# Interleaving a pair's two heads by row in the transposed scores, and making their pads on GpSimd

## The chip, the cores and the metric

The kernel runs on one core of a Trainium2 chip. A core has five engines that work side by side, each with its own queue of instructions: TensorE (PE) multiplies matrices and writes its results to PSUM; VectorE (DVE), ScalarE (ACT) and GpSimd (POOL) work on tiles in SBUF, and the first two on PSUM too; SyncE (SP) issues nearly all of this kernel's DMA transfers between SBUF and HBM. They are ordered against each other by semaphores only. Before a matmul TensorE loads a weight tile of up to 128x128 (the row PEld), which overlaps with the matmul before it.

The metric is the device time of the kernel in microseconds (us); lower is better.

## The reference, cut to what matters

Two mixers over the same 2048 rows of 512 features are blended by a gate:

```python
g = sigmoid((x * gate_w).sum(-1, keepdims=True))
a = Real(DFT_seq(DFT_hid(x)))            # matmuls with four DFT matrices
b = windowed_attention(x, wqkv, wo)      # 32 heads of 16, window 256, causal
out = g * a + (1 - g) * b

# inside b, for each head:
scores = q @ k.T * 16 ** -0.5
mask = (i - j >= 0) & (i - j < 256)
p = softmax(where(mask, scores, -1e9)); o = p @ v
```

All of it is float32. The change concerns the attention alone.

## The kernel before, in words

**Heads and steps.** The 32 heads are taken as four groups `g` of four pairs `p` of two heads `h`. A step `n` is one block of 64 rows of one group: 4 x 32 = 128 steps. In a step each pair's two heads share one matmul. For this, a *pad* is made: a 128x128 weight tile per pair in which 64 columns hold head 0's data (and zeros in head 1's feature rows) and the other 64 columns hold head 1's. With the pad as weights and the whole ring of keys or queries streaming, one matmul gives the scores of both heads, head 0 in partitions 0 to 63, head 1 in 64 to 127.

**Two passes.** `s_pair(n, p)` computes scores by query: pad of q (`pads[0]`), up to 320 keys (line 356); VectorE adds the mask and takes the row's extremum (358), ScalarE the exponentials with their sum (361). Nineteen steps later (`LAG`), `t_pair(k, p)` computes the same scores transposed, by key: pad of k (`pads[1]`), up to 320 queries (439). The row extremum comes in through extra rows 96 to 99 of the ring of q (written back from DRAM), and extra rows of the pad of k hold ones for the head they belong to (`mrow`, 208). ScalarE's exponential then writes the probabilities `pt` (440). GpSimd zeroes with `affine_select` what the window excludes: the first 64 queries (445) and, for a full window, the last 64 (449). This is done after each second pair (`p` odd) for two pairs at once, separately for each head's 64 partitions.

**The product with v.** `v_load` brings four blocks of v by two DMAs, head 0 to partitions 0 to 63, head 1 to 64 to 127; `v_spread` copies each half on GpSimd into its own 16 columns of `vpad` (423), whose other columns were zeroed once (203). `pv` (466) multiplies `vpad` with `pt` for the steps finished, three to five steps after their t, four pairs in four column stripes of TensorE.

**Pads.** `make_pad(i, n)` (332 to 340) is called for pad n one step ahead. Each pad is two instructions, one for each head, multiplying by the 0/1 column `half`. VectorE makes all of them (339) but the second half of the t pads, which ScalarE makes (337). There are two buffers for each kind, so pad n overwrites the pad of step n-2.

**What sets the order.** TensorE's order is written out by hand (`manual_schedule`): in the loop over n and p, `s_pair`, a quota of matmuls of the dense stream (`fill`: projections, then the DFT over rows, `dc`, line 518), `t_pair`, and again a quota; 16 dense matmuls a step while s runs, 12 after it. After step 127 of s only t and the dense stream remain for 19 steps, and then the DFT and the output projection alone. The orders on VectorE, ScalarE, GpSimd and SP come from a planner that simulates the engines; a few instructions are tied behind others (`behind`).

Of the kernel before, what the change touches and what calls it, by code (L numbers as in the profile page):

```python
# [7 lines left out]
F32 = mybir.dt.float32  # L8
F32R = mybir.dt.float32r
AF = mybir.ActivationFunctionType  # L10
OP = mybir.AluOpType
# [3 lines left out]
P = 128  # L15
# [5 lines left out]
BQ = 64  # L21
NB = S // BQ
WIN = 320
# [9 lines left out]
def fnet_window_mix(ctx: ExitStack, tc: tile.TileContext, xT, x, wqk, wv, wr, wi, cr, ci, wo, gw, out):  # L33
    nc = tc.nc

    const = ctx.enter_context(tc.tile_pool(name="const", bufs=1))
# [11 lines left out]
    v_scr = [dram.tile([2, P, 2, NG, 64], F32, name=f"v_scr{i}") for i in range(8)]  # L48
# [6 lines left out]
    def ld(dst, src):  # L55
        mark("sp", nc.sync.dma_start(dst, src))

    def f(ap):
        return ap.bitcast(F32)
# [4 lines left out]
    def mark(e, ins):  # L64
        last[e] = ins.ins

    @contextmanager
    def behind(*engines):
        with ExitStack() as es:
            for e in engines:  # L70
                if e in last:
                    es.enter_context(tc.issue_after(last[e]))
            yield
# [68 lines left out]
    with tc.manual_schedule(engines={mybir.EngineType.Activation, mybir.EngineType.DVE, mybir.EngineType.SP}):  # L142
# [12 lines left out]
        for dk in range(DK):  # L155
            c = slice(dk * 256, dk * 256 + 256)
# [7 lines left out]
    ring = [const.tile([P, NP, S], F32R, name=f"ring{i}") for i in range(2)]  # L164
# [3 lines left out]
    for h in (0, 64):  # L168
        m = mask[h:h + 64, :]
        nc.gpsimd.affine_select(m, m, pattern=[[1, WIN]], compare_op=OP.is_gt, fill=BIG,  # L170
                                base=0, channel_multiplier=-1)
        nc.gpsimd.affine_select(m, m, pattern=[[-1, WIN]], compare_op=OP.is_ge, fill=BIG,
                                base=256, channel_multiplier=1)
    ident = const.tile([P, P], F32R, name="ident")
    nc.gpsimd.memset(f(ident[:]), 1.0)
    nc.gpsimd.affine_select(ident[:], f(ident[:]), pattern=[[1, P]], compare_op=OP.is_equal, fill=0.0,
                            base=0, channel_multiplier=-1)

    half = const.tile([P, 2], F32, name="half")
    mrow = const.tile([P, 2], F32, name="mrow")  # L180
    for t, edges in ((half, ((0, 16, 32, 48, 64, 80), (16, 32, 48, 64, 80, 96))), (mrow, ((96, 98), (98, 100)))):
        nc.gpsimd.memset(t, 0.0)
        for h in range(2):
            for i, e in enumerate(edges[h]):
                a = t[:, h:h + 1]
                nc.gpsimd.affine_select(a, a, pattern=[[0, 1]], compare_op=OP.is_ge, fill=1.0 - i % 2,
                                        base=e - 1, channel_multiplier=-1)

    def clear_rows(i, ss):
        with behind("pool"):  # L190
            nc.gpsimd.memset(f(ring[i][96:128, :, ss * 512:(ss + 1) * 512]), 0.0)

    first_lo = f(XT[0, 0][96:128, 1]).rearrange("r (p c) -> r p c", p=NP)
    for t in pads[0]:
        mark("pool", nc.gpsimd.affine_select(t[96:128], first_lo, pattern=[[0, NP], [0, P]], compare_op=OP.is_gt,
                                             fill=0.0, base=0, channel_multiplier=0))
    clear_rows(1, 0)
    clear_rows(0, 0)
    vpad = [const.tile([P, 4, NP, 32], F32, name=f"vpad{b}") for b in range(2)]

    def clear_pads():
        for t in vpad:
            nc.gpsimd.memset(t, 0.0)
        for t in pads[1]:
            nc.gpsimd.memset(f(t[96:128]), 1.0)
            for h in range(2):
                a = t[96:128, :, 64 * h:64 * h + 64]
                nc.vector.tensor_scalar(a, f(a), mrow[96:128, h:h + 1], None, op0=OP.mult)


# [117 lines left out]
    def make_pad(i, n):  # L328
        if not 0 <= n < NG * NB:
            return  # L330
        t = pads[i][n % NPAD]
        b = n % NB
        with behind(*(("act", "dve") if n < NPAD else ())):
            for h in range(2):
                src, dst = f(ring[i][:96, :, b * BQ:(b + 1) * BQ]), t[:96, :, 64 * h:64 * h + 64]
                if i and h:
                    nc.scalar.activation(dst, src, AF.Copy, scale=half[:96, h:h + 1])  # L337
                else:
                    nc.vector.tensor_scalar(dst, src, half[:96, h:h + 1], None, op0=OP.mult)  # L339
        PAD[i, n] = t  # L340

    ML = {}
# [63 lines left out]
    def v_load(n):  # L406
        if n >= NG * NB:
            return
        g, kb = divmod(n, NB)
        raw = at.tile([P, 4, 64], F32, name="vr", bufs=1)  # L410
        for h in range(2):
            ld(raw[64 * h:64 * h + 64].rearrange("r (c j) x -> r c j x", j=2),
               v_scr[kb // 4][:, :, h, g, :].rearrange("c (j r) x -> r c j x", r=64))
        VR[n] = raw

    def v_spread(n):
        if n >= NG * NB:
            return
        raw = VR.pop(n)
        v2 = vpad[n // 4 % 2]  # L420
        for h in range(2):
            r = slice(64 * h, 64 * h + 64)
            nc.gpsimd.tensor_copy(v2[r, :, :, 16 * h:16 * h + 16], raw[r].rearrange("r j (p d) -> r j p d", d=16))  # L423
        V2[n // 4] = v2

    def t_pair(n, p):
        q0 = n % NB * BQ
        w = min(WIN, S - q0)
        if p == 0:
            if "proj" in have:  # L430
                more.append(n)
            c = (n - more[0]) % 6 * NP * WIN if more else 3072
            if c + NP * WIN <= 3072:
                PT[n] = f(home[:, c:c + NP * WIN].rearrange("p (a b) -> p a b", a=NP))
            else:
                PT[n] = at.tile([P, NP, WIN], F32, name="pt", bufs=4)
        pt = PT[n]
        ps = ps_a.tile([P, 512], F32, name="t", tag="st")
        nc.tensor.matmul(ps[:, :w], PAD[1, n][:, p], ring[0][:, p, q0:q0 + w], start=True, stop=True)  # L439
        nc.scalar.activation(pt[:, p, :w], ps[:, :w], AF.Exp, scale=-1.0)  # L440
        if p % 2:
            ph = slice(p - 1, p + 1)
            for h in (0, 64):
                a = pt[h:h + 64, ph, 0:64]
                nc.gpsimd.affine_select(a, a, pattern=[[0, 2], [1, 64]], compare_op=OP.is_ge, fill=0.0,  # L445
                                        base=0, channel_multiplier=-1)
                if w == WIN:
                    a = pt[h:h + 64, ph, 256:320]
                    nc.gpsimd.affine_select(a, a, pattern=[[0, 2], [-1, 64]], compare_op=OP.is_gt, fill=0.0,  # L449
                                            base=0, channel_multiplier=1)  # L450

    def pv(n):
        g, kb = divmod(n, NB)
# [375 lines left out]
    def v_next(n):  # L829
        if n < N:  # L830
            for c in range(2):
                need(("v", n % NB // 2 + c))
            with behind(*(("sp",) if n < 8 else ())):
                v_load(n)

    for n in range(N + LAG + 1):
# [3 lines left out]
        if n == 7:  # L840
            clear_pads()
        k = n - LAG
        ring_ahead(n + 1)
        if k in (-1, 4):
            v_spread(0 if k < 0 else 4)
        if k in (-4, -1, 4):
            v_next({-4: 0, -1: 4, 4: 8}[k])
        if n == 0:
            make_pad(0, 0)
        for p in range(NP):  # L850
            if n < N:
                s_pair(n, p)
            fill(n)
            if 0 <= k < N:
                t_pair(k, p)
            if p == 0:
                make_pad(0, n + 1)
                if k >= -1:
                    make_pad(1, k + 1)
            fill(n)  # L860
            for at_n, at_p, do in TURN:
                u, j = divmod(n - at_n, 8)
                if p == at_p and j == 0 and 0 <= u < 16:
                    do(u)
            if p == 3 and k % 8 == 6 and 0 <= k < N:
                l_load(k // 8)
            if p == 0 and full:
                o_out()
            if p == 2 and (k - summed >= (5 if more else 3) or k == N):
                for j in range(summed, k):  # L870
                    pv(j)
                summed = k
            if p == 3 and 4 * spread - 5 < summed and 4 * spread < N and n >= fresh:
                v_spread(4 * spread)
                spread += 1
                v_next(4 * spread)
                fresh = n + 2
# [49 lines left out]
```

## Time and profile before

| | |
|---|---|
| time, median of 3 runs | 855.69 us (852.19 to 856.47) |
| profiled execution, first to last instruction (span) | 854.1 us; the page gives no other time of it |
| busy: TensorE, VectorE, ScalarE, GpSimd | 844.2, 618.1, 592.0, 372.6 us |
| granted TensorE clock | 1.000 |
| t matmuls run | from 100.9 to 763.5 us |
| DMA | 161.04 MB, mean 189 GB/s |

A row of the profile's groups names the line, the engine, the operation, the tile written and the tiles read, the shapes (partitions x elements), the count, the busy time and mean of one, and the idle time of the engine ahead of them with what ended it. A matmul's recorded end is modelled, so consecutive records overlap, and the distance between two starts says more than a duration. Times on GpSimd are rough.

### The profile page before, as it was taken

To read this page: it belongs to the slowest core of one execution; us is meant where nothing else is said; L and a number is where in the kernel's file an instruction comes from. 1 tells how busy PE (TensorE), PEld (TensorE's weight loads), DVE (VectorE), ACT (ScalarE), POOL (GpSimd) and SP (SyncE) were. 2 spreads that over 40 slices of the span, in tenths; PEclk is the share of its full clock that TensorE was granted. 3 is DMA by queue.
4 is the path that set the end of the run, shared out by engine and by line. 5 is a ranking of instruction groups with operands and counts; after the bars stand their busy time and mean duration, and the time that the engine had idled before them with its cause. 6 is when DMAs were issued, how large, how long until landed. Compare 5 with 4: busy or idle time off the path is not lost.

```text
span 854.1 us, 17219 instructions
## 1 busy us (share of the span) xinstructions
PE 844.2 (99%) x5166; PEld 691.1 (81%) x5166; DVE 618.1 (72%) x2011; ACT 592.0 (69%) x1793; POOL 372.6 (44%) x1067
## 2 busy tenths in 40 slices
PE   8999999999999999999999999999999999999998
PEld 6788788788788888888878887788888887878876
DVE  5588978767879787669777787788988764447252
ACT  5388898888888987779778897678777765532020
POOL 9100254444542554555525555456355577830000
PEclk9999999999999999999999999999999999999999
DMA  7976577576665274444445447979784344339563
GB/s 240 289 234 201 177 253 239 203 240 216 205 233 188 52 221 129 145 121 151 138 133 143 158 150 228 267 264 298 246 232 136 119 154 133 130 119 289 148 188 133
DMA packets 94862, 161.04 MB, mean 189 GB/s; under 512 B 27312, under 2 KB 36272, under 8 KB 94768
## 3 DMA queue, kind: packets, MB, share of 16 engines
q1 hardware_dynamic: 94336, 159.28, 59.4%
q8 instruction: 40, 0.66, 0.3%
q10 hardware_dynamic: 432, 0.66, 0.2%
q14 instruction: 54, 0.44, 0.2%
HBM read 108.27 MB, written 51.64 MB: 187 GB/s over the span
## 4 chain that ended last, share of the span: by engine, by line
PE 92%; DVE 3%; DMA 3%; issue 1%; ACT 1%; SPq 0%; DVEq 0%; ACTq 0%
PE dc L518 40%; PE dab L294 10%; PE s L356 8%; PE t L439 8%; PE o L466 8%; PE dqk L271 8%; PE t L785 5%; PE dv L294 4%; DMA raw<-cr 1%; DMA raw<-xT 1%; DVE sm L358 1%; DMA pt<-wqk 1%; DVE pad L339 0%; DVE big L81 0%; DVE lo L574 0%
## 5 line engine op out<-in xcount | busy, mean ns | idle before, releaser
L361 ACT ACTIVATE sm<-sm,ml 128x320 f32<-128x320 f32 (+4 forms) x512 | 277.9, 544 | 102.7 <-DVE ml L358 97.3
L518 PE MATMUL dc<-big,hi 128*128 128x512 f32 x1020 | 344.1, 393 | 0.0
L358 DVE CUSTOM_DVE_ANT_0 sm<-s,mask 128x320 f32<-128x320 f32 (+4 forms) x512 | 235.3, 464 | 110.5 <-PE s L356 88.0
L445 POOL TENSOR_SCALAR_AFFINE_SELECT pt<-pt 64x128 f32<-64x128 f32 x392 | 136.1, 347 | 224.0 <-ACT pt L440 212.4
L518 PE MATMUL dc<-big,lo 128*128 128x512 f32 x510 | 200.5, 393 | 0.0
L518 PEld LDWEIGHTS dc<-big,hi 128*128 128x128 f32 x1020 | 179.7, 188 | 21.3
L440 ACT ACTIVATE pt<-t 128x320 f32<-128x320 f32 (+4 forms) x392 | 160.2, 411 | 43.5 <-PE t L439 41.1
L356 PE MATMUL s<-ring,pad 128*128 128x320 f32 (+4 forms) x512 | 157.7, 308 | 0.1
L439 PE MATMUL t<-ring,pad 128*128 128x320 f32 (+4 forms) x512 | 154.3, 301 | 0.4 <-DVE ml L358 0.4
L339 DVE TENSOR_SCALAR pad<-ring,half 96x256 fp32r<-96x256 f32 x384 | 119.8, 358 | 13.4 <-PE t L439 13.2
L449 POOL TENSOR_SCALAR_AFFINE_SELECT pt<-pt 64x128 f32<-64x128 f32 x344 | 121.7, 354 | 0.1
L356 PEld LDWEIGHTS s<-ring,pad 128*128 128x128 f32 x512 | 96.1, 188 | 30.2 <-issue 9.0
L439 PEld LDWEIGHTS t<-ring,pad 128*128 128x128 f32 x512 | 96.1, 188 | 22.4 <-DVE ml L358 1.6
L518 PEld LDWEIGHTS dc<-big,lo 128*128 128x128 f32 x510 | 95.9, 188 | 13.7 <-issue 1.6
L574 DVE TENSOR_TENSOR lo<-raw,hi 128x512 fp32r<-128x512 f32 x142 | 97.9, 698 | 0.1
L361 ACT ACTIVATION_READ_ACCUMULATOR sm<-sm,ml 128x1 f32 x512 | 97.5, 190 | 0.0
L294 PE MATMUL dab<-hi,big 128*128 128x512 f32 x256 | 89.1, 394 | 0.0
L271 PE MATMUL dqk<-big,hi 128*128 128x512 f32 x240 | 85.7, 394 | 1.3 <-DVE big L81 0.6
L423 POOL COPY vpad<-vr 64x256 f32<-64x256 f32 x64 | 26.9, 420 | 110.2 <-DMA vr<-v_scr 80.5
L574 DVE CAST hi<-raw 128x512 fp32r<-128x512 f32 x142 | 60.9, 438 | 17.4 <-PE dc L518 12.1
L445 POOL TENSOR_SCALAR_AFFINE_SELECT home<-home 64x128 f32<-64x128 f32 x120 | 45.1, 376 | 56.5 <-ACT home L440 49.0
L337 ACT ACTIVATE pad<-ring,half 96x256 fp32r<-96x256 f32 x128 | 63.8, 499 | 0.0
(96 smaller groups left out, 957.5 us busy)
## 6 DMA issues: line engine op xcount, KB each, us to landing
qk_scr<-home SPq DMA_DIRECT2D x32, 512.0 KB
ring<-qk_scr SPq DMA_DIRECT2D x32, 512.0 KB
raw<-cr SPq DMA_DIRECT2D x32, 512.0 KB
raw<-ci SPq DMA_DIRECT2D x32, 512.0 KB
r_scr<-ev SPq DMA_DIRECT2D x42, 256.0 KB
ev<-r_scr SPq DMA_DIRECT2D x42, 256.0 KB
ab_scr<-home SPq DMA_DIRECT2D x20, 512.0 KB
big<-ab_scr SPq DMA_DIRECT2D x20, 512.0 KB
```

What stands on the lines that cost most here:

```text
L271: nc.tensor.matmul(ps, w[a][:, c:c + 128], XT[dk, ss][:, b], start=n == 0, stop=n == 11)
L294: nc.tensor.matmul(ps, XT[dk, ss][:, a, c * 128:(c + 1) * 128], wh[b], start=n == 0, stop=n == 11)
L339: nc.vector.tensor_scalar(dst, src, half[:96, h:h + 1], None, op0=OP.mult)
L356: nc.tensor.matmul(ps[:, :w], PAD[0, n][:, p], ring[1][:, p, k0:k0 + w], start=True, stop=True)
L358: mark("dve", nc.vector.tensor_tensor_reduce(out=sm[:, :w], in0=ps[:, :w], in1=mask[:, WIN - w:], scale=1.0, scalar=3e38, op0=OP.add, op1= ...
L361: mark("act", nc.scalar.activation(sm[:, :w], sm[:, :w], AF.Exp, bias=nm[:, c], scale=-1.0, accum_out=l[:, c]))
L439: nc.tensor.matmul(ps[:, :w], PAD[1, n][:, p], ring[0][:, p, q0:q0 + w], start=True, stop=True)
L440: nc.scalar.activation(pt[:, p, :w], ps[:, :w], AF.Exp, scale=-1.0)
L445: nc.gpsimd.affine_select(a, a, pattern=[[0, 2], [1, 64]], compare_op=OP.is_ge, fill=0.0, base=0, channel_multiplier=-1)
L449: nc.gpsimd.affine_select(a, a, pattern=[[0, 2], [-1, 64]], compare_op=OP.is_gt, fill=0.0, base=0, channel_multiplier=1)
L518: nc.tensor.matmul(ps, w[a][:, i % 8 * 128:i % 8 * 128 + 128], ab[SC[i]][:, b], start=i == ends[0] and a + b == 0, stop=i == ends[1] and a ...
L574: return fn(*args)
```

## The change

- In the transposed scores a pair's two heads alternate by partition: partition 2r+h is key r of head h, where it was 64h+r. The pad of k is written with every second column (`turned`), and so are its extra rows.
- One `affine_select` over all 128 partitions masks both heads: its pattern steps by 2 where it stepped by 1, with the bases moved by one. The same selection on four quarters becomes one on two.
- Both halves of each t pad are made on GpSimd (`nc.gpsimd.tensor_scalar` by `half`), in place of VectorE and ScalarE. The pads of q stay on VectorE as they were.
- v is loaded by one DMA of 128 partitions in place of two of 64, its rows alternating by head. `v_spread` multiplies all 128 partitions by a 0/1 column `side` for each head's 16 columns, so that zeros are written each time, and the two memsets of `vpad` go.
- `side` is computed on VectorE at the start from the identity matrix: column 0 is one in even partitions, column 1 in odd ones.

```diff
@@ -178,6 +178,7 @@
 
     half = const.tile([P, 2], F32, name="half")
     mrow = const.tile([P, 2], F32, name="mrow")
+    side = const.tile([P, 2], F32, name="side")
     for t, edges in ((half, ((0, 16, 32, 48, 64, 80), (16, 32, 48, 64, 80, 96))), (mrow, ((96, 98), (98, 100)))):
         nc.gpsimd.memset(t, 0.0)
         for h in range(2):
@@ -186,6 +187,13 @@
                 nc.gpsimd.affine_select(a, a, pattern=[[0, 1]], compare_op=OP.is_ge, fill=1.0 - i % 2,
                                         base=e - 1, channel_multiplier=-1)
 
+    nc.vector.reduce_sum(side[:, 0:1], f(ident[:]).rearrange("p (r h) -> p h r", h=2)[:, 0],
+                         axis=mybir.AxisListType.X)
+    nc.vector.tensor_scalar(side[:, 1:2], side[:, 0:1], -1.0, 1.0, op0=OP.mult, op1=OP.add)
+
+    def turned(t):
+        return t[:].rearrange("x p (r h) -> x p r h", h=2)
+
     def clear_rows(i, ss):
         with behind("pool"):
             nc.gpsimd.memset(f(ring[i][96:128, :, ss * 512:(ss + 1) * 512]), 0.0)
@@ -199,12 +207,10 @@
     vpad = [const.tile([P, 4, NP, 32], F32, name=f"vpad{b}") for b in range(2)]
 
     def clear_pads():
-        for t in vpad:
-            nc.gpsimd.memset(t, 0.0)
         for t in pads[1]:
             nc.gpsimd.memset(f(t[96:128]), 1.0)
             for h in range(2):
-                a = t[96:128, :, 64 * h:64 * h + 64]
+                a = turned(t)[96:128, :, :, h]
                 nc.vector.tensor_scalar(a, f(a), mrow[96:128, h:h + 1], None, op0=OP.mult)
 
 
@@ -332,11 +338,11 @@
         b = n % NB
         with behind(*(("act", "dve") if n < NPAD else ())):
             for h in range(2):
-                src, dst = f(ring[i][:96, :, b * BQ:(b + 1) * BQ]), t[:96, :, 64 * h:64 * h + 64]
-                if i and h:
-                    nc.scalar.activation(dst, src, AF.Copy, scale=half[:96, h:h + 1])
+                src = f(ring[i][:96, :, b * BQ:(b + 1) * BQ])
+                if i:
+                    nc.gpsimd.tensor_scalar(turned(t)[:96, :, :, h], src, half[:96, h:h + 1], None, op0=OP.mult)
                 else:
-                    nc.vector.tensor_scalar(dst, src, half[:96, h:h + 1], None, op0=OP.mult)
+                    nc.vector.tensor_scalar(t[:96, :, 64 * h:64 * h + 64], src, half[:96, h:h + 1], None, op0=OP.mult)
         PAD[i, n] = t
 
     ML = {}
@@ -408,9 +414,8 @@
             return
         g, kb = divmod(n, NB)
         raw = at.tile([P, 4, 64], F32, name="vr", bufs=1)
-        for h in range(2):
-            ld(raw[64 * h:64 * h + 64].rearrange("r (c j) x -> r c j x", j=2),
-               v_scr[kb // 4][:, :, h, g, :].rearrange("c (j r) x -> r c j x", r=64))
+        ld(raw.rearrange("r (c j) x -> r c j x", j=2),
+           v_scr[kb // 4].rearrange("c (j r) h g x -> g (r h) c j x", r=64)[g])
         VR[n] = raw
 
     def v_spread(n):
@@ -419,8 +424,8 @@
         raw = VR.pop(n)
         v2 = vpad[n // 4 % 2]
         for h in range(2):
-            r = slice(64 * h, 64 * h + 64)
-            nc.gpsimd.tensor_copy(v2[r, :, :, 16 * h:16 * h + 16], raw[r].rearrange("r j (p d) -> r j p d", d=16))
+            nc.gpsimd.tensor_scalar(v2[:, :, :, 16 * h:16 * h + 16], raw.rearrange("r j (p d) -> r j p d", d=16),
+                                    side[:, h:h + 1], None, op0=OP.mult)
         V2[n // 4] = v2
 
     def t_pair(n, p):
@@ -440,14 +445,13 @@
         nc.scalar.activation(pt[:, p, :w], ps[:, :w], AF.Exp, scale=-1.0)
         if p % 2:
             ph = slice(p - 1, p + 1)
-            for h in (0, 64):
-                a = pt[h:h + 64, ph, 0:64]
-                nc.gpsimd.affine_select(a, a, pattern=[[0, 2], [1, 64]], compare_op=OP.is_ge, fill=0.0,
-                                        base=0, channel_multiplier=-1)
-                if w == WIN:
-                    a = pt[h:h + 64, ph, 256:320]
-                    nc.gpsimd.affine_select(a, a, pattern=[[0, 2], [-1, 64]], compare_op=OP.is_gt, fill=0.0,
-                                            base=0, channel_multiplier=1)
+            a = pt[:, ph, 0:64]
+            nc.gpsimd.affine_select(a, a, pattern=[[0, 2], [2, 64]], compare_op=OP.is_ge, fill=0.0,
+                                    base=1, channel_multiplier=-1)
+            if w == WIN:
+                a = pt[:, ph, 256:320]
+                nc.gpsimd.affine_select(a, a, pattern=[[0, 2], [-2, 64]], compare_op=OP.is_gt, fill=0.0,
+                                        base=-1, channel_multiplier=1)
 
     def pv(n):
         g, kb = divmod(n, NB)
```

## The prediction

> **What bounds the kernel now.** I read the page's first part, then the busy time by stage, the waits of TensorE, one step of its timeline, and last the groups of instructions that the change touches. Page and stages (columns of the stages: stretch, length, busy time of PE, PEld, DVE, ACT and POOL with instruction counts, granted clock, DMA share, GB/s):
>
> ```profile
> PE 844.2 (99%) x5166; PEld 691.1 (81%) x5166; DVE 618.1 (72%) x2011; ACT 592.0 (69%) x1793; POOL 372.6 (44%) x1067
> ```
> ```profile
> 60.00:100.00 40.00, 38.87 (x189) 32.66 (x187) 36.16 (x139) 33.70 (x101) 0.79 (x2) 1.00 0.58 186
> 100.00:200.00 100.00, 100.00 (x630) 82.16 (x630) 77.11 (x276) 86.47 (x271) 46.49 (x152) 1.00 0.70 229
> 500.00:600.00 100.00, 99.43 (x671) 80.94 (x670) 79.09 (x271) 75.03 (x240) 56.30 (x154) 1.00 0.79 242
> 700.00:720.00 20.00, 20.00 (x164) 16.19 (x160) 10.33 (x21) 10.72 (x25) 16.74 (x45) 1.00 0.48 165
> ```
>
> In the stages shown from 100 us on, TensorE is idle for 0.57 us of 220, at granted clock 1.00, while the other three have room. Matmul records overlap, so "busy" alone proves little; the timeline of one step (one block of 64 rows, loop over `p`) is the better witness:
>
> ```profile
> 384.03 0.31 PE L356 MATMUL s<-ring,pad 128*128 128x320 f32 x1
> 384.18 0.62 PE L518 MATMUL dc<-big,hi 128*128 128x512 f32 x2
> 384.63 0.31 PE L439 MATMUL t<-ring,pad 128*128 128x320 f32 x1
> 384.78 0.39 PE L518 MATMUL dc<-big,lo 128*128 128x512 f32 x1
> ...
> 388.83 0.31 PE L356 MATMUL s<-ring,pad 128*128 128x320 f32 x1
> ```
>
> A 128x512 matmul is followed after 0.225 us (the pair from 384.18 to 384.63 takes 0.45), a 128x320 one after 0.15. A step holds four s, four t and, with a fill of 4 a pair, 16 dense matmuls: 8 x 0.15 + 16 x 0.225 = 4.80 us, and the step takes 388.83 - 384.03 = 4.80. So TensorE streams without a gap; freeing VectorE or ScalarE shortens nothing there. What can be won is where TensorE does wait. Of its waits, those that start from the engines the change relieves:
>
> ```profile
> PE dqk L271 <- DVE home L86: 0.6, 1, 0.6
> PE s L376 <- DVE mlh L370: 0.5, 1, 0.5
> PE t L439 <- DVE ml L358: 0.4, 1, 0.4
> ```
>
> Together 1.5 us: that much is within the change's reach.
>
> **The change part by part.** The groups it touches (busy us, mean ns, idle before), and two that serve as scales:
>
> ```profile
> L445 POOL TENSOR_SCALAR_AFFINE_SELECT pt<-pt 64x128 f32<-64x128 f32 x392 | 136.1, 347 | 224.0 <-ACT pt L440 212.4
> L449 POOL TENSOR_SCALAR_AFFINE_SELECT pt<-pt 64x128 f32<-64x128 f32 x344 | 121.7, 354 | 0.1
> L445 POOL TENSOR_SCALAR_AFFINE_SELECT home<-home 64x128 f32<-64x128 f32 x120 | 45.1, 376 | 56.5 <-ACT home L440 49.0 <-PE dc L518 2.7
> L449 POOL TENSOR_SCALAR_AFFINE_SELECT home<-home 64x128 f32<-64x128 f32 x104 | 39.3, 377 | 0.0
> L423 POOL COPY vpad<-vr 64x256 f32<-64x256 f32 x64 | 26.9, 420 | 110.2 <-DMA vr<-v_scr 80.5 <-PE o L466 13.5 <-issue 7.7
> L195 POOL TENSOR_SCALAR_AFFINE_SELECT pad<-big 32x512 fp32r<-32x512 f32 x2 | 1.7, 858 | 0.1
> L176 POOL TENSOR_SCALAR_AFFINE_SELECT ident<-ident 128x128 fp32r<-128x128 f32 x1 | 0.3, 292 | 0.1
> ```
> ```profile
> L339 DVE TENSOR_SCALAR pad<-ring,half 96x256 fp32r<-96x256 f32 x384 | 119.8, 358 | 13.4 <-PE t L439 13.2
> L337 ACT ACTIVATE pad<-ring,half 96x256 fp32r<-96x256 f32 x128 | 63.8, 499 | 0.0
> ```
>
> *Selections.* 960 become 480, each over 128 partitions with the same 128 elements a partition. That doubled partitions cost nothing is seen at L176: 128x128 in 292 ns, no more than the 64x128 ones. GpSimd loses half of 136.1 + 121.7 + 45.1 + 39.3 = 342.2 us, that is 171.
>
> *Pads of t.* 128 instructions leave VectorE (128 x 358 ns = 46 us) and 128 leave ScalarE (63.8 us); 256 of 96x256 come to GpSimd, with every second element written. No row shows this operation there. Nearest are the COPY of 256 elements (420 ns) and the selection of 512 (858 ns). Bounds: 0.36 us, VectorE's own price for the same instruction, and 0.86, a pad as dear as twice its elements in a selection; I take 0.5, the COPY plus something for the multiplier column. Sum 256 x 0.5 = 128 us (92 to 220). The second half of a pad also waits for the first on the same engine, as the program order with its semaphores shows; I allow 0.1 us, nothing to 0.2.
>
> *Spread of v.* 64 copies over half the partitions become 64 multiplications over all of them, same 256 elements: +0.08 us each at the pad's price, 5 us (-4 to +28). The two memsets of the pads at the start go, 1.2 us off the path. In return VectorE computes `side` at the start: two instructions over at most 64 elements. They wait for GpSimd's identity:
>
> ```profile
> 2.46 0.29 POOL L176 TENSOR_SCALAR_AFFINE_SELECT ident<-ident 128x128 fp32r<-128x128 f32 x1
> ...
> 4.35 0.43 DVE L80 CAST big<-pt 128x512 fp32r<-128x512 f32 x1 [2.88 <-DMA pt<-xT]
> ```
>
> From 2.75 to 4.35 us VectorE has nothing but a DMA to wait for; two instructions that each stay below the 0.36 of a 256-element one end by 3.6, so the cost is nothing; without that cover it would be 0.7 us, once.
>
> *Loads of v.* 64 DMA issues of 64 KB become 32 of 128 KB on SP, same 256-byte pieces. At 0.61 us an issue SP gets up to 20 us back, or nothing if one issue takes twice as long; SP sets no end here.
>
> ```profile
> L56 SPq DMA_DIRECT2D vr<-v_scr x64: 574/609/1440, 87.2 to 726.6; - x64
> ```
>
> GpSimd's sum: 372.6 - 171 + 128 + 5 - 1 = 334 us (289 to 449): it does not become busier. But its work changes kind. Selections feed `pv`, which runs three to five steps later; a pad feeds the very next t. So GpSimd's delays, free until now, get a deadline, and this is where a loss would come from.
>
> *The deadline.* Pad n goes into the buffer that t of block n-2 reads, so it can start when t(n-2, p=3) is done, and must stand at t(n, p=0): five quarters of a step later, 1.25 x 4.80 = 6.0 us, less the 0.31 of the matmul. In the changed program's order on GpSimd, pad n stands between the first and the second selection pair of block n-2, so nothing that waits for a later exponential is ahead of it. It takes 2 x 0.5 + 0.1 = 1.1 us, which leaves 4.5 us. What is queued ahead can be a spread of v that waits for its DMA; the worst such case:
>
> ```profile
> 412.02 0.39 POOL L423 COPY vpad<-vr 64x256 f32<-64x256 f32 x1 [3.92 <-PE dc L518]
> ```
>
> GpSimd stands still for 3.92 us, with the spread's 2 x 0.5 it is 4.9 us, more than 4.5 by 0.4. Such a wait for the load of v occurs four times by L423's row (80.5 us, most of it one wait ahead of the first block), so three times later, and only hurts where the pad comes right behind. I charge nothing, bound 3 x 0.4 = 1.2 us.
>
> *Relief.* One visible stall is a t waiting behind pads on VectorE, after late chirp data:
>
> ```profile
> 546.07 0.43 DVE L574 CAST hi<-raw 128x512 fp32r<-128x512 f32 x1 [1.52 <-DMA raw<-cr]
> 546.41 0.87 DVE L339 TENSOR_SCALAR pad<-ring,half 96x256 fp32r<-96x256 f32 x3
> ```
> ```profile
> 546.90 0.39 PE L518 MATMUL dc<-big,lo 128*128 128x512 f32 x1
> 547.74 0.42 PE L439 MATMUL t<-ring,pad 128*128 128x320 f32 x1 [0.45 <-DVE ml L358]
> ```
>
> t comes 0.84 us after the matmul before it instead of 0.225: 0.6 us lost, of which I give back all; of the 1.1 us between 60 and 100 us, in which VectorE is busy 36.16 of 40, 0.4. Sum: 1.0 us less, -1.5 to +1.2.
>
> *A rule against the change.* Stretched instructions are seen on both engines: GpSimd's selections have a median of 292 ns but a mean of 347, and VectorE's casts and subtractions spread as well.
>
> ```profile
> L445 POOL TENSOR_SCALAR_AFFINE_SELECT pt<-pt x392: 286/292/1140, 103.3 to 764.3; 64x128 f32<-64x128 f32 x196
> ...
> L574 DVE CAST hi<-raw x142: 408/422/552, 70.3 to 824.3; 128x512 fp32r<-128x512 f32 x142
> L574 DVE TENSOR_TENSOR lo<-raw,hi x142: 619/686/810, 72.1 to 825.8; 128x512 fp32r<-128x512 f32 x142
> ```
>
> On VectorE the most that one of the 284 loses is 0.19 us, 54 us in all if each lost it; the pads give back 46, and VectorE at 77 to 79% has the rest idle. On GpSimd the stretch is 347/292 = 1.19, which makes a pad of 0.5 one of 0.6. Neither changes the sum. The Trainium skill, SBUF — State Buffer, in the section "SBUF: two separate sides", says that GpSimd and a VectorE instruction in a two-port mode, or with two SBUF inputs, lock each other out of a shared pair of ports for a whole instruction; the spreads above agree with it as far as they go, and what it would make of the pads is rival 1.
>
> **The rivals.**
> 1. *GpSimd's pads are late: slower.* It decides where GpSimd's work exceeds a step. Most steps: four selections at 0.3, two pads X with their 0.1, half a spread instruction (0.25): 4.80 = 1.55 + 2X, X = 1.6. The last stage has no s and a fill of 3: 4 x 0.15 + 12 x 0.225 = 3.30 us a step, and every fifth step its pv:
>
> ```profile
> 698.89 2.85 PE o L466 x64
> ...
> 718.47 2.83 PE o L466 x48
> ```
>
> Five steps in 718.47 - 698.89 = 19.6 us, 3.9 on the mean: X = 1.18. Some 19 steps lie there (LAG). A pad at the bound of 0.86, stretched by 1.19, is 1.02 and still fits. If each pad also waits out a subtraction of 0.69 on VectorE, X = 0.86 + 0.69 = 1.55 and the stage loses 19 x 2 x 0.37 = 14 us: 869; a loss over 0.5% begins at X = 1.3. For it: the operation's price is unknown, GpSimd was busy 16.74 of 20 us in this stage, VectorE's two-input instructions run all through it. Against: the COPY at 420 ns met the same neighbours. The lock named above is this rival's mechanism. The Trainium skill, GPSIMD Engine Reference, "Performance versus the Vector engine", measures GpSimd at about half of VectorE's speed in a two-input addition; carried over to this one it gives an estimate of 2 x 0.36 = 0.72 us, and the sum would be the same. Chance 0.11.
> 2. *VectorE's and ScalarE's relief is worth more than TensorE's gaps show, faster.* 110 us of work leave them. But all of TensorE's idle time is 854.1 - 844.2 = 9.9 us, and only 1.1 + 0.6 of it lies in the stages shown between 60 and 600. To gain 4.3 us, gaps hidden inside the busy records would have to go, and the step of 4.80 leaves none. 850. Chance 0.05.
> 3. *Order shifts*: with other engine loads SP's loads of chirp data move by a place or two and a wait like the one at 546 us grows or splits; +-2 us, inside the forecast.
>
> **How the numbers follow.** The profiled span is 854.1 us; the page gives no further time of that execution, and the median of the runs, 855.69, is 1.6 above it. Span less 1.0 is 853.1, and the same offset gives 854.7. Runs of before reach from 852.19 to 856.47, so 0.5% (4.3 us) is about what a measurement here can tell from no change. No change within it: 0.84, own range 852 to 857.5. Rival 1 with 0.11 pulls the upper end to 860, rival 2 the lower to 851.
>
> **What would show it.** Right: the t pads on GpSimd at 0.4 to 0.7 us, half as many selections at 0.29 to 0.35 each, VectorE near 570 us and ScalarE near 528 busy, TensorE still at 844 with a 4.80 step, no t waiting on GpSimd. Wrong: a wait of t for the pad on GpSimd in the list of TensorE's waits, above all from 700 us on; a pad over 1 us; a step over 4.80; selections over 128 partitions at twice the time.

## The result

The changed kernel takes 867.38 us (median, 865.82 to 868.07) where the kernel before, on the same chips, takes 856.08: a ratio of 1.0122, 95% interval 1.009 to 1.0155. It is slower by 1.2%, outside the forecast's range. The profiled execution of the changed kernel took 867.68 us, its span 865.9.

The changed kernel's busy time by engine, from its page, and its stages, over the same stretches that the prediction shows for the kernel before:

```profile
PE 855.5 (99%) x5166; PEld 691.7 (80%) x5166; DVE 617.9 (71%) x1885; ACT 554.2 (64%) x1665; POOL 519.1 (60%) x841
```
```profile
60.00:100.00 40.00, 39.41 (x189) 32.68 (x187) 35.83 (x137) 33.10 (x101) 1.84 (x2) 1.00 0.57 185
100.00:200.00 100.00, 98.73 (x612) 79.13 (x613) 73.25 (x250) 78.87 (x244) 62.94 (x112) 1.00 0.71 227
500.00:600.00 100.00, 100.00 (x627) 81.94 (x626) 81.09 (x256) 72.03 (x227) 74.45 (x121) 1.00 0.78 240
700.00:720.00 20.00, 20.00 (x148) 15.95 (x147) 11.70 (x22) 9.05 (x22) 19.09 (x33) 1.00 0.51 158
```

TensorE's busy time grew by 11.3 us, as much as the span (11.8), with the same 5166 matmuls at a granted clock of 1.00. So the loss isn't idle time: the same work takes TensorE longer. One step of its timeline (start, duration, engine, line), in the same block of rows as the step that the prediction showed at 4.80 us, counted here from the block's last pair on:

```profile
392.48 0.31 PE L362 MATMUL s<-ring,pad 128*128 128x320 f32 x1
392.63 0.39 PE L522 MATMUL dc<-big,lo 128*128 128x512 f32 x1
392.86 0.40 PE L522 MATMUL dc<-big,hi 128*128 128x512 f32 x1
393.10 0.31 PE L444 MATMUL t<-ring,pad 128*128 128x320 f32 x1
...
397.39 0.31 PE L362 MATMUL s<-ring,pad 128*128 128x320 f32 x1
```

From 392.48 to 397.39 is 4.91 us. No row reports a wait; the dense matmuls from 392.63 on follow each other after 0.23 and 0.24 us where it had been 0.225. Between the first t and the last, which the page of before has at 100.9 and 763.5 and this trace at 101.3 and 776.3, the loss is 12.4 us, all of it (the span grew by 11.8). Behind the attention the dense matmuls are as fast as ever:

```profile
784.61 0.61 PE L522 MATMUL dc<-big,hi 128*128 128x512 f32 x2
785.07 0.39 PE L522 MATMUL dc<-big,lo 128*128 128x512 f32 x1
785.29 0.61 PE L522 MATMUL dc<-big,hi 128*128 128x512 f32 x2
```

Three of them take 0.68 us, 0.227 each, as in the kernel before (0.68 us from 804.66 to 805.34).

The groups that the change touched:

```profile
L343 POOL TENSOR_SCALAR pad<-ring,half 96x256 fp32r<-96x256 f32 x256 | 279.7, 1106 | 93.5 <-PE t L444 80.1
L427 POOL TENSOR_SCALAR vpad<-vr,side 128x256 f32<-128x256 f32 x64 | 61.4, 971 | 104.0 <-DMA vr<-v_scr 65.1
L345 DVE TENSOR_SCALAR pad<-ring,half 96x256 fp32r<-96x256 f32 x256 | 109.3, 466 | 0.0
L449 POOL TENSOR_SCALAR_AFFINE_SELECT pt<-pt 128x128 f32<-128x128 f32 x196 | 70.8, 361 | 52.5 <-ACT pt L445 52.0
```

A pad half costs GpSimd 1.1 us, more than twice the 0.5 forecast. That invites the second explanation, late pads. The list of TensorE's waits has one, and the timeline shows it:

```profile
PE t L444 <- POOL pad L343: 1.4, 1, 1.4
...
PE t L444 <- ACT pt L445: 0.8, 1, 0.8
```
```profile
739.30 2.01 POOL L343 TENSOR_SCALAR pad<-ring,half 96x256 fp32r<-96x256 f32 x2
...
741.36 0.19 PEld L444 LDWEIGHTS t<-ring,pad 128*128 128x128 f32 x1 [1.79 <-POOL pad L343]
741.37 0.41 PE L444 MATMUL t<-ring,pad 128*128 128x320 f32 x1 [1.36 <-POOL pad L343]
```

About 2 us of the 12 are waits (1.4 + 0.8). The other 10 have no releaser.

### The profile page after: what moved, and what is told of

Read it like the earlier page. It is cut to its first block, busy times and chain, and to the rows that moved or that the text cites. A ratio compares the mean times of both kernels' runs of the same rounds, so it can differ in the third digit from the quotient of the medians.

```text
span 865.9 us, 16671 instructions
## 1 busy us (share of the span) xinstructions
PE 855.5 (99%) x5166; PEld 691.7 (80%) x5166; DVE 617.9 (71%) x1885; ACT 554.2 (64%) x1665; POOL 519.1 (60%) x841
## 4 chain that ended last, share of the span: by engine, by line
PE 88%; DMA 5%; DVE 3%; issue 1%; ACT 1%; SPq 0%; POOL 0%; DVEq 0%; ACTq 0%
PE dc L522 40%; PE dab L300 10%; PE s L362 8%; PE t L444 8%; PE o L470 8%; PE dqk L277 7%; PE dv L300 4%; PE t L789 3%; DMA out<-ev 1%; DMA ev<-o_scr 1%; DMA raw<-xT 1%; DMA qk_scr<-home 1%; DVE sm L364 1%; DMA pt<-wqk 0%; DVE big L81 0%
## 5 line engine op out<-in xcount | busy, mean ns | idle before, releaser
L522 PE MATMUL dc<-big,hi 128*128 128x512 f32 x1020 | 348.2, 396 | 0.0
L343 POOL TENSOR_SCALAR pad<-ring,half 96x256 fp32r<-96x256 f32 x256 | 279.7, 1106 | 93.5 <-PE t L444 80.1
L522 PE MATMUL dc<-big,lo 128*128 128x512 f32 x510 | 202.6, 397 | 0.0
L427 POOL TENSOR_SCALAR vpad<-vr,side 128x256 f32<-128x256 f32 x64 | 61.4, 971 | 104.0 <-DMA vr<-v_scr 65.1
L345 DVE TENSOR_SCALAR pad<-ring,half 96x256 fp32r<-96x256 f32 x256 | 109.3, 466 | 0.0
L449 POOL TENSOR_SCALAR_AFFINE_SELECT pt<-pt 128x128 f32<-128x128 f32 x196 | 70.8, 361 | 52.5 <-ACT pt L445 52.0
L578 DVE TENSOR_TENSOR lo<-raw,hi 128x512 fp32r<-128x512 f32 x142 | 100.9, 720 | 0.1
L578 DVE CAST hi<-raw 128x512 fp32r<-128x512 f32 x142 | 65.2, 468 | 34.3 <-PE dc L522 29.1
L453 POOL TENSOR_SCALAR_AFFINE_SELECT pt<-pt 128x128 f32<-128x128 f32 x172 | 63.5, 369 | 0.0
L445 ACT ACTIVATE home<-t 128x320 f32<-128x320 f32 (+4 forms) x120 | 48.8, 409 | 17.6 <-PE t L444 17.0
```

What stands on the lines that cost most here:

```text
L343: nc.gpsimd.tensor_scalar(turned(t)[:96, :, :, h], src, half[:96, h:h + 1], None, op0=OP.mult)
L345: nc.vector.tensor_scalar(t[:96, :, 64 * h:64 * h + 64], src, half[:96, h:h + 1], None, op0=OP.mult)
L449: nc.gpsimd.affine_select(a, a, pattern=[[0, 2], [2, 64]], compare_op=OP.is_ge, fill=0.0, base=1, channel_multiplier=-1)
L522: nc.tensor.matmul(ps, w[a][:, i % 8 * 128:i % 8 * 128 + 128], ab[SC[i]][:, b], start=i == ends[0] and a + b == 0, stop=i == ends[1] and a ...
L578: return fn(*args)
```

## The experiments

Three causes were put against each other. *Layout (A):* the new tile `side`, 8 bytes a partition, takes a slot of 32 bytes in SBUF, by the addresses in the built programs; `vpad`, `home` and the pools `big`, `st`, `ev` and `at`, all allocated after it, lie 32 bytes further, while the pads and rings ahead of it stay. *GpSimd's work (B)* slows TensorE's streaming. *Late pads (C)* make it wait.

**e1: the change with the old layout.**

```diff
-    half = const.tile([P, 2], F32, name="half")
-    mrow = const.tile([P, 2], F32, name="mrow")
+    both = const.tile([P, 4], F32, name="half")
+    half, mrow = both[:, 0:2], both[:, 2:4]
```

> The changed kernel with half and mrow in one tile of 16 bytes, so that side takes up no new 32-byte slot and every later tile lies where it lay before the change (at a multiple of 64 bytes in the partition; in the changed kernel they lie 32 bytes off). Computes the same. Theory A (the layout: the new tile moves the dense operands by 32 bytes, and each 128x512 matmul streams 4 to 5 ns slower while the attention runs): 856 us, +-2, the 512-column matmuls back at a mean distance near 228.5 ns between 110 and 690 us. Theory B (GpSimd's longer work, 519 us against 373, slows TensorE's streaming): 867 us, 232.7 ns. Theory C (pads late): 867 us, too, but with waits of t for the pads of several us.

857.65 us, ratio 1.0026 (1.0009 to 1.0043). The page and one step:

```profile
PE 845.9 (99%) x5166; PEld 690.9 (81%) x5166; DVE 616.9 (72%) x1885; ACT 551.4 (65%) x1665; POOL 520.2 (61%) x841
```
```profile
384.80 0.31 PE L362 MATMUL s<-ring,pad 128*128 128x320 f32 x1
384.95 0.62 PE L522 MATMUL dc<-big,hi 128*128 128x512 f32 x2
385.40 0.31 PE L444 MATMUL t<-ring,pad 128*128 128x320 f32 x1
...
389.60 0.31 PE L362 MATMUL s<-ring,pad 128*128 128x320 f32 x1
```

GpSimd is as busy as in the changed kernel (520.2 against 519.1 us), yet the step is back at 4.80. B and C fall as the main cause.

**e2: the kernel before with an unused slot.**

```diff
     mrow = const.tile([P, 2], F32, name="mrow")
+    gap = const.tile([P, 2], F32, name="gap")
+    nc.vector.memset(gap, 0.0)
```

> The kernel before with an unused tile of 8 bytes (a 32-byte slot) behind mrow, filled once by VectorE; nothing else. Theory A: 866 us, +-3, 512-column matmuls at 232 to 233 ns. Theory B and C: 855.7 us, 228.4 ns.

866.92 us, ratio 1.0121 (1.0086 to 1.0155): the whole loss, with nothing of the change in it. The step:

```profile
390.22 0.31 PE L358 MATMUL s<-ring,pad 128*128 128x320 f32 x1
...
395.12 0.31 PE L358 MATMUL s<-ring,pad 128*128 128x320 f32 x1
```

4.90 us. With e1, this shows A from both sides.

**e3: the t pads made on VectorE and ScalarE again, layout as changed.**

```diff
-                if i:
-                    nc.gpsimd.tensor_scalar(turned(t)[:96, :, :, h], src, half[:96, h:h + 1], None, op0=OP.mult)
+                if i and h:
+                    nc.scalar.activation(turned(t)[:96, :, :, h], src, AF.Copy, scale=half[:96, h:h + 1])
+                elif i:
+                    nc.vector.tensor_scalar(turned(t)[:96, :, :, h], src, half[:96, h:h + 1], None, op0=OP.mult)
```

> The changed kernel with the t pads made as before, first half on VectorE, second on ScalarE, still interleaved; the layout stays the changed one (32 bytes off). Theory A: 866 us, +-3. Theory B: 856, with GpSimd at some 250 us of work. Theory C: 856.

866.76 us, ratio 1.0122 (1.0101 to 1.0143), as by A: taking the pads off GpSimd doesn't help while the layout is wrong. Its row for the pads of q, which stay on VectorE throughout:

```profile
L347 DVE TENSOR_SCALAR pad<-ring,half 96x256 fp32r<-96x256 f32 x256 | 81.1, 357 | 0.0
```

357 ns, where the changed kernel has 466 beside GpSimd's pads.

**e4: the kernel before with the t pads on GpSimd alone.**

```diff
-                if i and h:
-                    nc.scalar.activation(dst, src, AF.Copy, scale=half[:96, h:h + 1])
+                if i:
+                    nc.gpsimd.tensor_scalar(dst, src, half[:96, h:h + 1], None, op0=OP.mult)
```

> The kernel before with one thing of the change: both halves of the t pads on GpSimd, heads still in two blocks; selections, v and layout as before. GpSimd's work then is 373 us and some 256 pads at 1.0 us, 620 us. Theory A: 856 us and what late pads cost where GpSimd's eight selections a step and two pads fill a step, above all after 700 us: 857 to 866. Theory B: more than 867, since GpSimd is busier than in the changed kernel.

872.61 us, ratio 1.021 (1.0162 to 1.0259). By the time alone B would have been right, and A's upper end of 866 was missed. The profile tells them apart; waits (of the whole run) and busy time in the last stage of t:

```profile
L337 POOL TENSOR_SCALAR pad<-ring,half 96x256 fp32r<-96x256 f32 x256 | 268.6, 1059 | 47.1 <-PE t L439 30.8
```
```profile
PE t L439 <- POOL pad L337: 9.1, 8, 2.9
PE o L466 <- POOL pt L445: 2.2, 1, 2.2
```
```profile
700.00:782.00 82.00, 70.69 (x483) 52.56 (x476) 23.41 (x40) 26.36 (x65) 74.49 (x167) 0.98 0.35 114
```

In this stretch TensorE is idle for 11.3 of 82 us, GpSimd busy for 74.49: rival 1 of the prediction in full, with the named waits. Ahead of it the step is 4.80 us (the median, as in the kernel before), which B can't explain. The pads here are written in two blocks and cost 1059 ns: writing every second element isn't what makes them dear. And the halved selections are what makes room for the pads: with both, in e1, two microseconds are lost; without them, 17, although e4 still has the cheaper spread of v.

**f1 and f2: which operands?** A one-tile pool of 32 bytes behind `big`; in f1 it moves `hi`, `lo` (the weights of the DFT's dense matmuls) and what lies behind them, the other engines' tiles included; f2 merges `half` and `mrow` as well, so that `big` (what is streamed) with `home` and `vpad` lies 32 bytes lower and the rest as before.

```diff
     big = ctx.enter_context(tc.tile_pool(name="big", bufs=16))
+    gapp = ctx.enter_context(tc.tile_pool(name="gapp", bufs=1))
...
+    gap = gapp.tile([P, 2], F32, name="gap")
+    nc.vector.memset(gap, 0.0)
```

> The kernel before with an unused 32-byte slot between the pools big and st: the dense matmuls' weight tiles hi and lo, and ev, pt, sm behind them, lie 32 bytes off a multiple of 64; the streamed tiles (big), home and vpad lie as before. Theory A1 (the streamed operand's place sets the speed): 856 us, +-2, 512-column matmuls at 228.5 to 229.5 ns. Theory A2 (the place of the weights does, or that of the tiles of the other engines): 866 us, +-3, 232 to 234 ns.

> The kernel before with half and mrow in one 16-byte tile, and the 32 bytes put back behind the pool big: big (the streamed operand of the DFT), home and vpad lie 32 bytes off a multiple of 64, hi, lo, ev, pt and sm as before. Theory A1: 866 us, +-3, 512-column matmuls at 232 to 234 ns. Theory A2: 856 us, +-2. If both shifts cost half, each alone gives 861.

864.56 us, ratio 1.0093 (1.006 to 1.0125), and 864.15, ratio 1.0092 (1.006 to 1.0125). Neither theory holds: each shift alone costs most of the whole, and they don't add up. The traces say why. Behind the attention, where dense matmuls run alone, f1 is slow too:

```profile
784.63 0.63 PE L521 MATMUL dc<-big,hi 128*128 128x512 f32 x2
785.09 0.40 PE L521 MATMUL dc<-big,lo 128*128 128x512 f32 x1
785.33 0.63 PE L521 MATMUL dc<-big,hi 128*128 128x512 f32 x2
```
```profile
785.00:788.00 3.00, 3.00 (x15) 2.41 (x14) 0.85 (x2) 0.00 (x0) 0.00 (x0) 1.00 0.82 222
```

Three take 0.70 us, 0.233 each, where the changed kernel takes 0.227, with ScalarE and GpSimd idle and VectorE busy for 0.85 of 3 us. f2 does the same (0.70 us from 786.36 to 787.06); in the other runs the median behind the attention is 227 ns. So f1 and f2 each change two distances: the one between a dense operand and the rings, and the one between a dense matmul's own streamed and weight tiles, which e2 leaves as it was. The second costs without any alternation.

**g1: dense operands at multiples of 128 bytes.** Leaving out one 64-byte tile moves `big` and all behind it from odd multiples of 64 to multiples of 128.

```diff
-            e = const.tile([P, 16], F32, name="ge")
+            e = g0
```

> The kernel before with the gate's helper tile ge put into g0, which takes 64 bytes out: big, hi, lo, ev, pt and sm then lie at multiples of 128 bytes, where before they lie at odd multiples of 64. If the unit that counts is 64 bytes: 855.7, +-1.5, and 512-column matmuls at 229 ns. If it is 128 bytes: these go towards the 227 ns that they take behind the attention, and the time to some 851.

864.5 us, ratio 1.0094 (1.0062 to 1.0126). The rounder addresses are the slower ones: alignment of a tile by itself, which e1 and e2 had suggested, is not it either.

**g2: the change without its pads, in the old layout** (the edits of e1 and e3 together).

> The changed kernel with the layout of before (half and mrow in one tile) and the t pads on VectorE and ScalarE again; the single selections, the spread by multiplication and the interleaved heads stay. What is left of the change then frees GpSimd (some 250 us of work against 373) and touches nothing TensorE waits for: 855.7, +-2. If selections or the spread had been what cost the aligned changed kernel its 0.26%, it stays at 857.7.

856.7 us, ratio 0.9992 (0.9968 to 1.0016): no difference that shows from the kernel before, although GpSimd does a third less (250.9 us). What e1 still loses points to the pads on GpSimd: the intervals of e1 and g2 overlap a little, but in the traces e1 takes 76.8 us from the last s to the last t, with TensorE idle for 1.25 of them, where g2 and the kernel before take 75.3 with no idle time. Nothing else of the change costs or brings anything that shows.

**h2, h3, h4: place, or place relative to what?** For the loss during the attention, what is left is that TensorE alternates between two families of operands: pads and rings (s, t), and dense ones. h2 puts a 32-byte slot ahead of the pads, so that everything moves together; h3 does so and merges `half` and `mrow`, so that only pads and rings move; h4 only merges, so that the dense side moves 32 bytes down.

```diff
+    gap = const.tile([P, 2], F32, name="gap")
+    nc.vector.memset(gap, 0.0)
     NPAD = 2
```

> The kernel before with an unused 32-byte slot ahead of the pads: every tile, the pads and rings of the attention and the dense operands alike, lies 32 bytes further. Theory R (what counts is where the dense operands lie relative to the pads and rings, between which TensorE alternates): 856 us, +-2, a 512-column matmul in front of a t or s at 226 ns. Theory Q (the dense operands' own place counts): 866, +-3, 232 to 237 ns, as with the slot behind mrow.

> The kernel before with the slot ahead of the pads and half and mrow in one tile: pads and rings lie 32 bytes further, vpad, home, big, hi, lo and all behind them where they lay before. Theory R: slow, 862 to 867, although no dense operand has moved. Theory Q: 856, +-2.

> The kernel before with half and mrow in one tile and nothing added: all dense operands lie 32 bytes lower, pads and rings as before. By theory R the distance is the same as with the rings 32 bytes further, so both agree within 2 us and in the distances between matmuls; by theory Q this one is slow (862 to 867) and that one isn't.

h2: 856.31 us, ratio 1.0003 (0.9984 to 1.0023). h3: 863.62, ratio 1.0087 (1.0062 to 1.0113). h4: 860.02, ratio 1.0047 (1.0026 to 1.0069). A step of h2 and one of h3:

```profile
384.27 0.31 PE L358 MATMUL s<-ring,pad 128*128 128x320 f32 x1
...
389.07 0.31 PE L358 MATMUL s<-ring,pad 128*128 128x320 f32 x1
```
```profile
386.16 0.30 PE L358 MATMUL s<-ring,pad 128*128 128x320 f32 x1
...
391.01 0.30 PE L358 MATMUL s<-ring,pad 128*128 128x320 f32 x1
```

Moved together, 4.80 us although every address is new; with the rings moved alone, 4.85, although no dense operand has moved. h3 and h4 agree in the step (4.85) and in the time of the last t (768.1 and 767.5 us), as theory R has it; their totals differ by 3.6 us, more than the 2 expected. That arises behind the attention, where h3's output projection also works in the moved ring slots (`fin`, `os`); 1.2 us of it is a longer wait for VectorE, the rest is open.

All layouts in one table; shifts in bytes against the kernel before, the step is the median over steps without a pv from block 60 on, so it doesn't order the totals exactly; each ratio is to the kernel before in runs beside it (medians 855.58 to 856.36 us):

| kernel | pads, rings | `big` | `hi`, `lo` | step, us | median, us | ratio |
|---|---|---|---|---|---|---|
| h2 | +32 | +32 | +32 | 4.80 | 856.31 | 1.0003 |
| e1 (changed kernel) | 0 | 0 | 0 | 4.80 | 857.65 | 1.0026 |
| h4 | 0 | -32 | -32 | 4.85 | 860.02 | 1.0047 |
| h3 | +32 | 0 | 0 | 4.85 | 863.62 | 1.0087 |
| f2 | 0 | -32 | 0 | 4.88 | 864.15 | 1.0092 |
| f1 | 0 | 0 | +32 | 4.91 | 864.56 | 1.0093 |
| e2 | 0 | +32 | +32 | 4.91 | 866.92 | 1.0121 |
| changed | 0 | +32 | +32 | 4.91 | 867.38 | 1.0122 |
| g1 | 0 | -64 | -64 | 4.94 | 864.50 | 1.0094 |

The distances between starts, which the expectations name, sort the runs in much the same way. From 110 to 690 us a 512-column matmul is followed after 228 ns (median, worked out from the traces) in the kernel before, e1, e4, g2 and h2, after 231 in h3 and h4, and after 233 in the changed kernel, e2, e3, f1, f2 and g1. Ahead of an s or t it is 226 ns in h2, as theory R has it, and 231 in both h3 and h4.

Of six relative placements tried (h3 and h4 have the same one but for the output projection), the one of the kernel before is the fastest. No version beat the kernel before. Not tested by itself: in all these runs the tiles that the other engines use (`raw`, `ev`, `pt`, `sm`) move together with `hi` and `lo`, so the part of these accesses during the attention is open. How much GpSimd works, at least, makes no difference: 250.9 us in g2, 520.2 in e1 and 625.5 in e4, each with a step of 4.80.

## Why the prediction was wrong

- *What bounds the kernel* was right: TensorE, at 99% before and after. The relief of the other engines bought nothing that shows, neither GpSimd's (g2) nor ScalarE's (551.4 us in e1); the 1.0 us that the prediction gave for it is too small to be told here. Rival 2 was rightly held to be unlikely.
- *The step that failed* stands under the spread of v: `side` was costed as two instructions on VectorE, "so the cost is nothing". They cost nothing; the place that the tile takes costs 11.3 us in e2, as much as the whole loss. The prediction took the 0.225 and 0.15 us between matmuls for properties of the matmul. They depend on where its operands and its neighbours' lie as well, so the step of 4.80, in which "TensorE streams without a gap", was the best of several possible values (4.80 to 4.94) and not a floor that only others' waits could raise. No rival asked what could make TensorE itself slower. The measured 867.38 lies near rival 1's 869 by coincidence: two of rival 1's signs came (a pad over 1 us, a wait of t for a pad), but in e1, which keeps both, only 0.26% is lost.
- *The pad's price* was mis-sized: 0.5 taken, 0.36 to 0.86 bounded, 1.11 measured on the mean, outside the bounds; the 0.72 estimated from a two-input addition falls short as well. A COPY (420 ns) and a selection are no scale for a multiplication by a column on GpSimd; the spread of v, the same 256 elements, went from 420 to 971 ns with that operation. The sum for GpSimd, 334 us with an upper end of 449, came out at 519.
- *Rival 1's point of decision* (X = 1.18 in the last stage, a loss of 0.5% from X = 1.3) was about right, in part because errors cancelled: a spread instruction took 0.97 us where 0.5 was put in, and the last blocks need fewer selections. With the pad at 1.11 on the mean a wait of 1.4 us shows in that stage, and the change in the old layout loses 0.26%. e4, with twice the selections, is over the point and loses 2.1%.
- *The selections* were right but for a little: 361 ns over 128 partitions, where 0.29 to 0.35 us was forecast, and half as many.
- *VectorE's relief* wasn't: forecast near 570 us, measured 617.9. The pads that stayed went from 358 to 466 ns, and from there back to 357 when GpSimd's pads were taken away (e3). The Trainium skill, SBUF — State Buffer, "SBUF: two separate sides", describes what could do this, the shared pair of ports that one of the two engines holds for a whole instruction; the times agree with it, though no run here shows the lock itself, and the prediction had weighed it on VectorE for casts and subtractions alone. It was still free, since VectorE isn't the bound. ScalarE, forecast near 528 us, came to 554.2: records of one engine overlap (the five largest groups of ScalarE in the kernel before add to 648 us, its busy time is 592.0), so a group's 63.8 us can't be taken off whole.
- *The deadline's worst case* was misread: the 3.92 us ahead of the COPY at 412.02 ended with a matmul (`<-PE dc L518`) and are not one of the four waits for the load of v. Nothing was charged for it, and no number of the forecast rests on it but the 1.2 us of its bound.
- *The start* was right: the first t comes at 101.3 us, 0.4 later than before.

## What to carry to other kernels

When one engine streams without gaps, compare the distances between its instructions' starts before and after, step by step: a loss with no wait and a busy time that grows as much as the span is in the instructions themselves. Adding a tile, however small (here 8 bytes), moves all that is allocated behind it; where TensorE is the bound, put new small tiles where nothing shifts, or into the slack of an existing one, and measure an unused slot of the same size as a control. And price an operation on GpSimd only by a row of that operation.

## What the runs showed of the hardware

TensorE's rate depends on where its operands lie relative to each other, and a shift of 32 bytes is enough to show it: the same program, with nothing but an unused 32-byte slot added, takes 1.2% longer when the slot lies between the rings and the dense operands, and the same time when it lies ahead of both. The cost is a few nanoseconds a matmul where matmuls of both families alternate (a step of 4 s, 4 t and 16 dense ones takes 4.80 to 4.94 us over the layouts); the changed kernel's dense matmuls behind the attention take 0.227 us each. Where the streamed and the weight tiles of the dense matmuls themselves are moved against each other by 32 bytes (f1, f2), these take 0.233 us even alone. The recorded clock stays between 0.998 and 1.000 on the mean, and no wait that would account for the loss is reported. What in the memory causes it, and for the loss during the attention which pair of operands (streamed against streamed, or against the weights being loaded) it is, the runs leave open.

A multiplication by a column on GpSimd takes 1.0 to 1.1 us for 256 elements over 96 or 128 partitions, in blocks (1059 ns) or with every second element (1106), where a COPY of 256 elements takes 0.42.
